# First-layer weights in two column halves, and one cast between two masks, in a fused retention and bilinear FFN kernel

## Chip, cores, metric

One core of a Trainium2 chip. The metric is the device time of one execution in microseconds (us), the median of several. A second number, the span of a profile, is counted from the first to the last instruction; it is about 1.7 us less than the time of the same execution.

## The reference

```python
# q, k, v: (8 batches, 8 heads, 576 positions, 64), float32; w_a, w_b: (512, 1536); w_out: (1536, 512)
scores = (1 / 8) * q @ k.T                            # per batch and head
D      = gamma_h ** (i - j) where i >= j, else 0      # gamma_h = 1 - 2 ** (-5 - h)
x      = (scores * D) @ v                             # heads side by side: (4608 tokens, 512)
out    = ((x @ w_a) * (x @ w_b)) @ w_out              # float32, (4608, 512)
```

## The kernel before

The tokens go through in 36 chunks of 128. Retention runs chunkwise: the decay is split into factors for q (applied to the output) and for v (applied when v is cast), and a running `state` carries the earlier chunks. The FFN runs in blocks of 512, 256, 384, 384, then 512 tokens. Chunks 0 to 3 are done first, in a prologue; the work of all later chunks is woven into the stream of FFN products at fixed places, counted in products of 512 columns.

The weights come by GpSimd DMAs that cast float32 to bf16 on the way, wa and wb in three pieces of 3, 4 and 5 column tiles of 128:

```python
def load_w(f0, f1):
    nc.gpsimd.dma_start(wa_sb[:, :, f0:f1], wa_r[:, :, f0:f1])
    nc.gpsimd.dma_start(wb_sb[:, :, f0:f1], wb_r[:, :, f0:f1])

def cast(i, on="pool"):                     # q, k to bf16; v to bf16 with its decay
    # [...] q on ScalarE (or GpSimd)
    if on == "dve":
        nc.vector.tensor_copy(kb, kf)
    else:
        nc.gpsimd.tensor_copy(kb, kf)
    nc.gpsimd.tensor_tensor(vb, vf, vs[...], op=ALU.mult)      # shapes cut

def scores(i):
    # [...] eight products into two PSUM tiles, then two masks, put off into `later`:
    later.append(lambda: masked(0))         # sT[:, 0] = ps[0] * mask, on VectorE
    later.append(lambda: masked(1))

# the prologue
for i in range(4):
    if idle[i][0]:
        warm(idle[i][0])                    # products without a use, which keep TensorE busy
    scores(i)
    flush()                                 # both masks
    if i == 2:
        load_w(0, W1)
        load_w(W1, W2)
    if i < 3:
        cast(i + 1, "dve" if i == 2 else "act")
    state(i)                                # needs vb of chunk i
    if idle[i][1]:
        warm(idle[i][1])
    if i < 3:
        transposes(i + 1)                   # needs q and k of chunk i+1 in bf16
        outputs(i)                          # needs both masks of chunk i; VectorE scales it into xT
        flush()
load_w(W2, DFF)
for i in (0, 1, 2):
    load_wo(i)
outputs(3, halves=True)
flush()
nc.sync.dma_start(gate, wo_sb[0:1, 3, 0:64])     # holds the loads behind it until W_out's first part is there
for i in range(4, 9):
    load(i)
```

In block 0 the products follow the pieces: with `WCOLS = [3, 4, 5]`, three column tiles of x·wa, the same three of x·wb, then four and four, then five and five. Each x·wa tile is copied to `ha` by ScalarE, and VectorE multiplies it with the x·wb tile into hT. All other blocks alternate wa and wb tile by tile.

Of the kernel before, what the change touches and what calls it, by code (L numbers as in the profile page):

```python
# [18 lines left out]
def kernel(  # L19
# [19 lines left out]
    nc = tc.nc  # L39
# [3 lines left out]
    DFF = moe_w_a.shape[1]  # L43
    NTOK = B * S
    NC = DM // 128
    NF = DFF // 128
# [19 lines left out]
    def pool(name, bufs, space=None):  # L66
        kw = {} if space is None else {"space": space}
        return ctx.enter_context(tc.tile_pool(name=name, bufs=bufs, **kw))
# [5 lines left out]
    qkt_pool = pool("qkt", 6)  # L74
    st_pool = pool("st", 4)
    h_pool = pool("hT", 2)
    ha_pool = pool("ha", 6)
    o_pool = pool("osb", 4)
    PS = bass.MemoryType.PSUM
    ps_ffn = pool("ps_ffn", 3, PS)  # L80
# [5 lines left out]
    wa_r = moe_w_a.rearrange("(c p) f -> p c f", p=128)  # L86
    wb_r = moe_w_b.rearrange("(c p) f -> p c f", p=128)
    wo_r = moe_w_out.rearrange("(c p) m -> p c m", p=128)
    wa_sb = big.tile([128, NC, DFF], BF16)
    wb_sb = big.tile([128, NC, DFF], BF16)  # L90
# [69 lines left out]
        nc.vector.memset(t, 0.0)  # L160

    def load_w(f0, f1):
        nc.gpsimd.dma_start(wa_sb[:, :, f0:f1], wa_r[:, :, f0:f1])
        nc.gpsimd.dma_start(wb_sb[:, :, f0:f1], wb_r[:, :, f0:f1])

    def load_wo(i):
        nc.gpsimd.dma_start(wo_sb[:, 4 * i:4 * i + 4, :],
# [6 lines left out]
    def pop():  # L174
        if later:
            later.pop(0)()

    def flush():
        while later:
            later.pop(0)()  # L180

    def cast(i, on="pool"):

        qf, kf, vf = staged.pop(i)
        qkb = nat.tile([128, 2, DM], BF16, tag="qkb", name="qkb")
        vb = nat.tile([128, DM], BF16, tag="vb", name="vb")
        qb, kb = qkb[:, 0], qkb[:, 1]
        if on == "pool":
            nc.gpsimd.tensor_copy(qb, qf)  # L189
        else:  # L190
            nc.scalar.copy(qb, qf)  # L191
# [4 lines that stand above are left out]
        nc.gpsimd.tensor_tensor(  # L196
            vb.rearrange("p (h d) -> p h d", h=H),
            vf.rearrange("p (h d) -> p h d", h=H),
            vs[:, i % PER, :].unsqueeze(2).to_broadcast([128, H, D]),
            op=ALU.mult)  # L200
        natural[i] = (qkb, qb, kb, vb)
# [9 lines left out]
    def transposes(i):  # L211

        natural_qk = natural[i][1:3]
        qkT = qkt_pool.tile([128, 2, HP, 128], BF16, tag="qkT", name="qkT")
        for w, copy in ((0, nc.scalar.copy), (1, nc.vector.tensor_copy)):
            tp = ps_att.tile([128, HP, 128], BF16, tag="att", name="tp")
            for p in range(HP):
                nc.tensor.transpose(tp[:, p, :],  # L218
                                    natural_qk[w][:, p * 128:(p + 1) * 128],
                                    identity)  # L220
            copy(qkT[:, w], tp)
        transposed[i] = qkT

    def state(i):
        m = i % PER
        if m == PER - 1:
            return
        qkb, qb, kb, vb = natural[i]
        r = slice(64, 128) if m == MID else slice(0, 128)
        if m == 0 or m == MID:  # L230
            kv_of[0] = ps_kv.tile([128, HP, 128], FP32, tag="kv", name="kv")
        kv = kv_of[0]
        for p in range(HP):
            sl = slice(p * 128, (p + 1) * 128)
            nc.tensor.matmul(kv[:, p, :], kb[r, sl], vb[r, sl],  # L235
                             start=(m in (0, MID) and p == 0), stop=True,
                             skip_group_check=True)
        st = states[i % len(states)]
        state_of[i + 1] = st
        nc.scalar.copy(st[0:64, :, 0:64], kv[0:64, :, 0:64])  # L240
        nc.scalar.copy(st[64:128, :, 64:128], kv[64:128, :, 64:128])

    def scores(i):
        qkT = transposed[i]
        ps = [ps_att.tile([128, HP, 128], FP32, tag="att", name=f"sc{hi}")
              for hi in (0, 1)]
        sT = st_pool.tile([128, 2, HP, 128], BF16, tag="sT", name="sT")
        scored[i] = sT
        for p in range(HP):
            for hi in (0, 1):  # L250
                r = slice(64 * hi, 64 * hi + 64)
                nc.tensor.matmul(ps[hi][:, p, :], qkT[r, 1, p, :],  # L252
                                 qkT[r, 0, p, :], start=True, stop=True,
                                 skip_group_check=True)
        keep = mask2 if i % PER == MID else mask

        def masked(hi):
            nc.vector.tensor_tensor(
                sT[:, hi], ps[hi],
                keep.unsqueeze(1).to_broadcast([128, HP, 128]),  # L260
                op=ALU.mult)

        later.append(lambda: masked(0))
        later.append(lambda: masked(1))

    def outputs(i, halves=False):
        m = i % PER
        qkb, qb, kb, vb = natural.pop(i)
        qkT = transposed.pop(i)
        sT = scored.pop(i)  # L270
        o = ps_att.tile([128, HP, 128], FP32, tag="att", name="o")
        if m > 0:
            st = state_of.pop(i)
            n = 64 if m == MID else 128
            for p in range(HP):
                for hi in (0, 1):
                    nc.tensor.matmul(o[64 * hi:64 * hi + 64, p, 0:n],  # L277
                                     st[:, p, 64 * hi:64 * hi + 64],
                                     qkT[:, 0, p, 0:n],
                                     start=(p == 0), stop=True,  # L280
                                     skip_group_check=True)
        for p in range(HP):
            for hi in (0, 1):
                e0 = p * 128 + 64 * hi
                nc.tensor.matmul(o[64 * hi:64 * hi + 64, p, :],  # L285
                                 vb[:, e0:e0 + 64], sT[:, hi, p, :],
                                 start=(m == 0 and p == 0), stop=True,
                                 skip_group_check=True)
        s0 = rows_of(i)[0][3]

        def scaled(c0, c1):
            nc.vector.tensor_tensor(  # L292
                xT[:, c0:c1, i * 128:(i + 1) * 128], o[:, c0:c1],
                qs[:, c0:c1, s0:s0 + 128], op=ALU.mult)

        if halves:
            later.append(lambda: scaled(0, HP // 2))
            later.append(lambda: scaled(HP // 2, HP))
        else:
            later.append(lambda: scaled(0, HP))  # L300


    blocks = [512, 256, 384, 384] + [512] * ((NTOK - 1536) // 512)
    WCOLS = [3, 4, 5]

    def ffn_block(tok0, n, runs):

# [60 lines left out]
    def warm(count):  # L368

        w = ps_ffn.tile([128, 4, 128], FP32, tag="ab", name="w")  # L370
        for _ in range(count):
            nc.tensor.matmul(w, identity,  # L372
                             identity.unsqueeze(1).to_broadcast([128, 4, 128]),
                             start=True, stop=True)

    W1, W2 = 128 * WCOLS[0], 128 * (WCOLS[0] + WCOLS[1])
    idle = {0: (0, 0), 1: (0, 3), 2: (2, 4), 3: (1, 4)}
    make_qs(0)
    make_qs(1)
# [4 lines left out]
    for i in range(4):  # L384
        if idle[i][0]:
            warm(idle[i][0])
        scores(i)
        flush()
        if i == 2:
            load_w(0, W1)  # L390
            load_w(W1, W2)
        if i < 3:
            cast(i + 1, "dve" if i == 2 else "act")
        state(i)
        if idle[i][1]:
            warm(idle[i][1])
        if i < 3:
            transposes(i + 1)
            outputs(i)
            flush()  # L400
    load_w(W2, DFF)
    for i in (0, 1, 2):
        load_wo(i)
    outputs(3, halves=True)
# [77 lines left out]
    at = 0.0  # L482
    tok = 0
    for tb, n in enumerate(blocks):
        runs = WCOLS if tb == 0 else [1] * NF
        for cost, edge in ffn_block(tok, n, runs):
            at += cost
            while todo and edge and at >= todo[0][0]:
                _, fn, args = todo.pop(0)
                fn(*args)  # L490
        flush()
        tok += n
# [30 lines left out]
```

## Time and profile before

| | us |
|---|---|
| median of three executions | 345.88 (345.83 to 346.28) |
| the execution that was profiled | 879.55, span 877.8 |

The first thing to read is that the profile is not a picture of the timed runs: the profiled execution took two and a half times as long. From the page of the kernel before, its span, its busy times and TensorE's row of the span in 40 slices (busy share in tenths):

```profile
span 877.8 us, 6134 instructions
...
PE 854.0 (97%) x2390; PEld 309.4 (35%) x2426; DVE 162.0 (18%) x272; ACT 112.6 (13%) x229; POOL 84.3 (10%) x121
...
PE   6999999999999999999999999999999999999998
```

TensorE (PE) seems full, and the summary of the chain of waits agrees (share of the span by engine):

```profile
PE 97%; issue 2%; DMA 1%; SPq 0%; POOL 0%; DVE 0%; ACT 0%
```

But the pace is wrong. From the same chain in order of time (start, duration, what), 20 products of block 0, each with 512 columns:

```profile
62.97 11.87 PE pa L316 x20
```

That is 0.59 us per product. The FFN has 1296 of these (nine times 512 tokens; per 512 tokens 12·4 for wa, 12·4 for wb and 48 for W_out), which alone makes over 760 us at this pace and cannot fit into 346. So every TensorE duration of this profile is useless for the timed runs.

What it does show is when the weights come. From the DMA issues of the kernel before (bytes as written in bf16, and us from issue to landing):

```profile
wa_sb<-in_moe_w_a_dram POOLq DMA_DIRECT2D x1, 640.0 KB, 12.0
wb_sb<-in_moe_w_b_dram POOLq DMA_DIRECT2D x1, 640.0 KB, 14.2
wa_sb<-in_moe_w_a_dram POOLq DMA_DIRECT2D x1, 512.0 KB, 8.9
wb_sb<-in_moe_w_b_dram POOLq DMA_DIRECT2D x1, 512.0 KB, 10.6
...
wa_sb<-in_moe_w_a_dram POOLq DMA_DIRECT2D x1, 384.0 KB, 6.0
wb_sb<-in_moe_w_b_dram POOLq DMA_DIRECT2D x1, 384.0 KB, 7.0
```

and GpSimd in order of time, from vb of chunk 2 to vb of chunk 3:

```profile
14.12 1.04 POOL L196 TENSOR_TENSOR vb<-vf,vs 128x512 bf16<-128x512 f32 x1 [0.61 <-DMA vf<-in_v_dram]
15.11 0.95 POOL L163 DMA_DIRECT2D wa_sb<-in_moe_w_a_dram  x1
16.05 0.76 POOL L164 DMA_DIRECT2D wb_sb<-in_moe_w_b_dram  x1
16.79 0.76 POOL L163 DMA_DIRECT2D wa_sb<-in_moe_w_a_dram  x1
17.52 0.77 POOL L164 DMA_DIRECT2D wb_sb<-in_moe_w_b_dram  x1
18.28 1.08 POOL L196 TENSOR_TENSOR vb<-vf,vs 128x512 bf16<-128x512 f32 x1
```

Adding the issue times gives landings of wa at 21.1, 25.7, 31.3 us and of wb at 23.0, 28.1, 34.5 us. Each weight DMA holds GpSimd for about 0.75 us, and vb of chunk 3 stands behind four of them.

### The profile page before, as it was taken

The page shows a single profiled execution, that of the slowest core. Times are in us where ns is not written, and L with a number is a line of the kernel's source. Part 1 is how long each engine was busy: PE and PEld are TensorE (multiplying, and loading weights), DVE is VectorE, ACT ScalarE, POOL GpSimd, SP SyncE. Part 2 cuts the span into 40 slices and gives each one's busy share as a digit, 9 for nine tenths or more (in the row PEclk, how much of TensorE's full clock was granted, in tenths as well). Part 3 has the DMA queues.
Part 4 walks back from the last instruction along what each step waited for, and adds up shares of the span by engine and source line. Part 5 has one row for each costly group of instructions (what it writes and reads, how often), then busy time and mean ns, then how long its engine had stood idle before and what let it go on. Part 6 is the DMA issues. An engine that isn't in the chain of part 4 may idle for free.

```text
span 877.8 us, 6134 instructions
## 1 busy us (share of the span) xinstructions
PE 854.0 (97%) x2390; PEld 309.4 (35%) x2426; DVE 162.0 (18%) x272; ACT 112.6 (13%) x229; POOL 84.3 (10%) x121
## 2 busy tenths in 40 slices
PE   6999999999999999999999999999999999999998
PEld 3322345344344333333333333432333333232223
DVE  4211122222121111211122112121121112201100
ACT  5111112011011101100111011101110011101110
POOL 6040002201011010002100210011000000000000
DMA  9980049350090041025400650066002300000000
GB/s 181 207 152 0 25 90 187 80 88 1 29 199 0 13 102 18 0 50 108 81 1 1 131 108 1 0 112 129 0 1 60 61 0 1 8 28 12 0 13 36
DMA packets 154333, 50.74 MB, mean 58 GB/s; under 512 B 144960, under 2 KB 149824, under 8 KB 154304
## 3 DMA queue, kind: packets, MB, share of 16 engines
q1 hardware_dynamic: 149552, 45.63, 26.6%
q0 software_dynamic: 4752, 4.72, 3.4%
q8 instruction: 19, 0.31, 0.2%
q14 instruction: 10, 0.08, 0.0%
HBM read 37.75 MB, written 9.44 MB: 54 GB/s over the span
## 4 chain that ended last, share of the span: by engine, by line
PE 97%; issue 2%; DMA 1%; SPq 0%; POOL 0%; DVE 0%; ACT 0%
PE pb L329 29%; PE pa L316 29%; PE po L349 28%; PE o L285 2%; PE kv L235 2%; PE o L277 2%; PE w L372 1%; PE tp L218 1%; DMA kf<-in_k_dram 1%; SPq L104 0%; POOL qkb L195 0%; PE sc_2460 L252 0%; PE sc_2449 L252 0%; PE sc_1402 L252 0%; PE sc_3677 L252 0%
## 5 line engine op out<-in xcount | busy, mean ns | idle before, releaser
L329 PE MATMUL pb<-xT,wb_sb 128*128 128x512 bf16 (+2 forms) x471 | 279.9, 775 | 2.7 <-issue 2.7
L316 PE MATMUL pa<-xT,wa_sb 128*128 128x512 bf16 (+2 forms) x472 | 277.3, 769 | 3.6 <-issue 3.1
L349 PE MATMUL po<-wo_sb,hT 128*128 128x512 bf16 (+1 forms) x425 | 253.2, 810 | 6.2 <-issue 6.2
L334 DVE TENSOR_TENSOR hT<-ha,pb 128x512 bf16<-128x512 bf16 (+2 forms) x120 | 76.2, 635 | 457.4 <-PE pb L329 443.3
L329 PEld LDWEIGHTS <-wb_sb 128*128 128x128 bf16 x480 | 82.8, 172 | 173.7 <-issue 168.0
L316 PEld LDWEIGHTS <-wa_sb 128*128 128x128 bf16 x480 | 80.7, 172 | 157.2 <-issue 151.4
L349 PEld LDWEIGHTS <-hT 128*128 128x128 bf16 x444 | 73.1, 169 | 162.1 <-issue 159.0
L322 ACT CAST ha<-pa 128x512 bf16<-128x512 f32 (+2 forms) x120 | 65.2, 544 | 447.1 <-PE pa L316 440.9
L196 POOL TENSOR_TENSOR vb<-vf,vs 128x512 bf16<-128x512 f32 x36 | 37.6, 1044 | 295.1 <-issue 144.3
L189 POOL CAST qkb<-qf 128x512 bf16<-128x512 f32 x30 | 18.3, 611 | 290.5 <-DMA qf<-in_q_dram 274.6
L360 DVE COPY osb<-po 128x512 f32<-128x512 f32 (+1 forms) x17 | 11.5, 676 | 175.5 <-PE po L349 175.5
L358 ACT COPY osb<-po 128x512 f32<-128x512 f32 (+1 forms) x20 | 11.5, 576 | 219.3 <-PE po L349 208.4
L292 DVE TENSOR_TENSOR xT<-o,qs 128x512 bf16<-128x512 f32 (+1 forms) x37 | 24.8, 674 | 46.8 <-PE o L285 46.8
L285 PE MATMUL o<-sT,vb 128*64 128x128 bf16 x288 | 30.4, 379 | 0.0
L235 PE MATMUL kv<-vb,qkb 128*128 128x128 bf16 (+1 forms) x128 | 25.4, 373 | 1.4 <-issue 0.9
L235 PEld LDWEIGHTS <-qkb 128*128 128x128 bf16 (+1 forms) x128 | 17.6, 161 | 22.2 <-issue 20.9
L285 PEld LDWEIGHTS <-vb 128*64 128x64 bf16 x288 | 22.3, 181 | 2.5 <-issue 2.5
L195 POOL CAST qkb<-kf 128x512 bf16<-128x512 f32 x32 | 19.7, 616 | 13.6 <-DMA kf<-in_k_dram 13.5
L252 PEld LDWEIGHTS <-qkT 64*128 64x128 bf16 x288 | 15.4, 135 | 12.6 <-issue 9.8
L218 PE MATMUL tp<-identity,qkb 128*128 128x128 bf16 x48 | 8.1, 362 | 6.0 <-ACT qkb L191 5.3
L372 PE MATMUL w<-identity 128*128 128x512 bf16 x14 | 9.3, 790 | 0.0
L218 PEld LDWEIGHTS <-qkb 128*128 128x128 bf16 x48 | 5.2, 140 | 11.1 <-ACT qkb L191 5.7
(195 smaller groups left out, 194.7 us busy)
## 6 DMA issues: line engine op xcount, KB each, us to landing
out_dram<-osb SPq DMA_DIRECT2D x35, 256.0 KB, 2.2
qf<-in_q_dram SPq DMA_DIRECT2D x32, 256.0 KB, 3.6
kf<-in_k_dram SPq DMA_DIRECT2D x32, 256.0 KB, 4.2
vf<-in_v_dram SPq DMA_DIRECT2D x32, 256.0 KB, 4.7
wo_sb<-in_moe_w_out_dram POOLq DMA_DIRECT2D x3, 512.0 KB, 17.8
qf<-in_q_dram SPq DMA_DIRECT2D x8, 128.0 KB, 3.6
kf<-in_k_dram SPq DMA_DIRECT2D x8, 128.0 KB, 3.5
vf<-in_v_dram SPq DMA_DIRECT2D x8, 128.0 KB, 3.5
```

Source lines behind the costliest of these rows:

```text
L189: nc.gpsimd.tensor_copy(qb, qf)
L195: nc.gpsimd.tensor_copy(kb, kf)
L196: nc.gpsimd.tensor_tensor(vb.rearrange("p (h d) -> p h d", h=H), vf.rearrange("p (h d) -> p h d", h=H), vs[:, i % PER, :].unsqueeze(2).to_ ...
L218: nc.tensor.transpose(tp[:, p, :], natural_qk[w][:, p * 128:(p + 1) * 128], identity)
L235: nc.tensor.matmul(kv[:, p, :], kb[r, sl], vb[r, sl], start=(m in (0, MID) and p == 0), stop=True, skip_group_check=True)
L285: nc.tensor.matmul(o[64 * hi:64 * hi + 64, p, :], vb[:, e0:e0 + 64], sT[:, hi, p, :], start=(m == 0 and p == 0), stop=True, skip_group_che ...
L292: nc.vector.tensor_tensor(xT[:, c0:c1, i * 128:(i + 1) * 128], o[:, c0:c1], qs[:, c0:c1, s0:s0 + 128], op=ALU.mult)
L316: nc.tensor.matmul(pa[:, 0:n], wa_sb[:, c, fs], xT[:, c, tok0:tok0 + n], start=(c == 0), stop=(c == NC - 1))
L322: nc.scalar.copy(ha[:, 0:n], pa[:, 0:n])
L329: nc.tensor.matmul(pb[:, 0:n], wb_sb[:, c, fs], xT[:, c, tok0:tok0 + n], start=(c == 0), stop=(c == NC - 1))
L334: nc.vector.tensor_tensor(hT[:, F, 0:n], has[F][:, 0:n], pb[:, 0:n], op=ALU.mult)
L349: nc.tensor.matmul(po[:, 0:width], hT[:, F, u * 128:(u + 1) * 128], wo_sb[:, F, cols], start=(F == 0), stop=(F == NF - 1))
```

## The change

Its intent, as the few words that came with it and the code show: load wa and wb in two halves, so that GpSimd has four weight DMAs to issue and not six; let only three of them stand ahead of vb of chunk 3; run block 0 as six wa tiles, six wb tiles, and again; and cast k of chunk 3 on VectorE between the two masks of chunk 2, so that its transposes can begin earlier. `ha` gets a seventh buffer for the longer run.

```diff
-    ha_pool = pool("ha", 6)
+    ha_pool = pool("ha", 7)
 [...]
     def load_w(f0, f1):
-        nc.gpsimd.dma_start(wa_sb[:, :, f0:f1], wa_r[:, :, f0:f1])
-        nc.gpsimd.dma_start(wb_sb[:, :, f0:f1], wb_r[:, :, f0:f1])
+        for w_sb, w_r in ((wa_sb, wa_r), (wb_sb, wb_r)):
+            nc.gpsimd.dma_start(w_sb[:, :, f0:f1], w_r[:, :, f0:f1])
+            yield
 [...]
-    WCOLS = [3, 4, 5]
+    WRUN = NF // 2
 [...]
         scores(i)
-        flush()
+        pop()
         if i == 2:
-            load_w(0, W1)
-            load_w(W1, W2)
-        if i < 3:
-            cast(i + 1, "dve" if i == 2 else "act")
+            list(load_w(0, W1))
+            second = load_w(W1, DFF)
+            next(second)
+        if i == 2:
+            cast(3, "dve")
+            flush()
+        else:
+            flush()
+            if i < 3:
+                cast(i + 1, "act")
 [...]
-    load_w(W2, DFF)
+    list(second)
 [...]
-        runs = WCOLS if tb == 0 else [1] * NF
+        runs = [WRUN] * 2 if tb == 0 else [1] * NF
```

The built instruction streams differ in just these places: the order of block 0's products, one cast and one mask swapped on VectorE, and GpSimd's DMAs.

More of the change, by code (lines that the diff above doesn't have):

```diff
@@ L374, in warm @@
                              start=True, stop=True)
-    W1, W2 = 128 * WCOLS[0], 128 * (WCOLS[0] + WCOLS[1])
+    W1 = 128 * WRUN
     idle = {0: (0, 0), 1: (0, 3), 2: (2, 4), 3: (1, 4)}
```

## The prediction

> **What bounds the kernel now.** The profile is unlike the timed runs: its span is 877.8 us, the timed median 345.88. The chain of waits is 97% TensorE, and block 0's products with 512 columns follow each other every 0.60 us (20 in 11.87 us). The FFN has 1296 such products: at 0.60 us they alone would be 778 us. The Trainium skill ("TensorE: Matmul & The Clock Gate", Back-to-back gap and its table) gives about 216 ns at full clock; 1296 of those are 280 us, which fits the timed runs. So I take matmul times from the skill, and every DMA, VectorE, ScalarE and GpSimd time from the trace. Timed runs are TensorE-bound too, except in the prologue (chunks 0 to 3), which is a chain of loads, casts, copies and masks. The change touches only that and block 0; later blocks keep their instruction order.
>
> **Weights, from the DMA issues and landings in the trace.** wa lands in pieces of 3, 4, 5 column tiles at 21.1, 25.7 and 31.3 us, wb at 23.0, 28.1 and 34.5; W_out at 37.0 to 42.3. Bytes flow at a steady ~207 GB/s, so landing is set by bytes ahead in the queue, not by TensorE.
>
> **Adds, removes, moves.**
> 1. Two of six GpSimd DMA issues go (0.76 us each). In the timeline vb of chunk 3 starts at 18.28 us after four issues, though its load landed at 17.4; after three issues it starts at about 17.5. State of chunk 3, the last four warming matmuls and the output of chunk 3 follow it: up to 0.75 us earlier.
> 2. VectorE: k of chunk 3 is cast (0.42 us) between two masks (0.6 us spacing). That can bring its transposes 0.6 us forward, but its load lands only at about 16.5 us (issue at 11.29 plus 5.2). With fast matmuls the first mask ends before that, I estimate, and VectorE then waits for the load with the second mask behind it: between 0.5 us gained and 0.35 us lost.
> 3. The first product now needs 768 KB of wa (bf16 as written) in place of 384 KB. These bytes were wa's and wb's first pieces together, landing at 23.0; with larger packets I expect 22.6 to 23.0.
> 4. The second half of the run order costs nothing: wb half 1 lands at ~26.9, wanted at ~28; wa half 2 at ~30.7, wanted at ~33.
>
> **Critical path.** Working through the prologue with full-clock matmuls I estimate block 0 starts at 21.5 us before (at half clock 22.9). After, attention would be ready at about 20.7 (22.1), but wa holds it until about 22.7. So block 0 starts 1.2 us later (or 0.2 us earlier), and everything behind moves with it.
>
> **Predicted time:** 346.4 us, range 344.9 to 347.9. Faster by over 2%: 1%; within 2%: 98%; slower by over 2%: 1%. Within that, slightly slower is likelier (65%).
>
> **What would show it.** wa's first landing near 22.8 us; vb of chunk 3 starting near 17.5; the VectorE cast of k waiting for its DMA or directly behind the first mask; at a fast clock the first pa product waiting for wa's DMA instead of the xT multiply. In a profile as slow as this one (block 0 starts at 29.5 us, well after the weights) the wait cannot appear, and the span should hardly change.
>
> **What would make it wrong.** A timed prologue longer than I estimate (block 0 starting after 23 us): then points 1 and 2 are real gains of 0.3 to 0.75 us. A larger first transfer ramping up faster. Or an idle TensorE that drops its clock at block 0, costing 1 to 2 us more.

## More of the kernel before

From chunk 6 on, q and k are transposed by DMA (`turn`), and the places of chunks 6 to 10 are:

```python
placed = [((6, 7), 145, 178, 194), ((8,), 166, 197, 207), ((9, 10), 186, 224, 254)]
# chunks: where the casts are issued, where the scores stand, where the outputs stand
```

## The result, and the profile after

| | kernel before | changed kernel |
|---|---|---|
| median, us | 345.90 (4 runs, 345.83 to 346.28) | 345.97 (4 runs, 345.51 to 347.08) |
| ratio | | 1.0004, 95% interval 0.998 to 1.0029 |

A ratio is the mean time of one kernel's fast runs over that of the other's fast runs of the same rounds, so it is not quite the ratio of the medians. The interval says: the same, within 0.3%, which is 1 us. Nearly all effects below are of that size or smaller, so most of the evidence is in the traces, not in the times.

The profile of the changed kernel fell in a fast execution (347.08 us), so TensorE's pace can now be read:

```profile
span 345.4 us, 6131 instructions
...
PE 328.0 (95%) x2390; PEld 171.8 (50%) x2426; DVE 160.8 (47%) x272; ACT 112.4 (33%) x229; POOL 83.5 (24%) x119
```

The chain of waits of the changed kernel around the start of block 0 (start, duration, what):

```profile
13.66 0.99 POOL vb L197
14.65 7.15 DMA wa_sb<-in_moe_w_a_dram
21.80 0.04 issue
21.84 0.39 PE pa L317
22.23 0.05 issue
22.29 4.91 PE pa L317 x22
```

The first product of block 0 waits for wa's half, which was issued at 14.65 us and lands at 21.80 us. The 22 products after it come every 0.22 us, so TensorE is at full clock. No VectorE or GpSimd step is in this chain any more between vb of chunk 2 and the first product. GpSimd in order of time shows that the intended gain is there: vb of chunk 3 stands behind three issues and starts at 17.15 us.

```profile
16.33 0.76 POOL L164 DMA_DIRECT2D wa_sb<-in_moe_w_a_dram  x1
...
17.15 1.04 POOL L197 TENSOR_TENSOR vb<-vf,vs 128x512 bf16<-128x512 f32 x1
```

VectorE in order of time has the cast of k between the two masks:

```profile
15.52 0.69 DVE L259 TENSOR_TENSOR sT<-sc_305,mask 128x512 bf16<-128x512 f32 x1 [0.17 <-PE sc_306 L253]
...
16.13 0.47 DVE L194 CAST qkb<-kf 128x512 bf16<-128x512 f32 x1
...
16.52 0.67 DVE L259 TENSOR_TENSOR sT<-sc_306,mask 128x512 bf16<-128x512 f32 x1
```

And these are TensorE's waits for DMAs in the whole changed kernel (us in total, times, longest):

```profile
PE pa L317 <- DMA wa_sb<-in_moe_w_a_dram: 1.7, 1, 1.7
PE sc_1216 L253 <- DMA qkT<-qkb: 1.4, 1, 1.4
...
PE sc_1399 L253 <- DMA qkT<-qkb: 0.7, 1, 0.7
...
PE sc_1111 L253 <- DMA qkT<-qkb: 0.5, 1, 0.5
```

The last three lines are the ones that I had not looked for: scores of chunks 8, 10 and 12 waited 2.6 us for DMA transposes, at 72, 80 to 82 and 94 us.

To follow a delay through the kernel I use the 120 hT multiplies of VectorE: they stand in each trace in the same order, and the start of the n-th in one trace less that of the n-th in another is the lag at this point. The lag below is always against the fast profile of the kernel before that the first experiment brought.

### The profile page after: what moved, and what is told of

Its sections match the earlier page's. It is cut to its first block, busy times and chain, and to the rows that moved or that the text cites. A ratio compares the mean times of both kernels' runs of the same rounds, so it can differ in the third digit from the quotient of the medians.

```text
span 345.4 us, 6131 instructions
## 1 busy us (share of the span) xinstructions
PE 328.0 (95%) x2390; PEld 171.8 (50%) x2426; DVE 160.8 (47%) x272; ACT 112.4 (33%) x229; POOL 83.5 (24%) x119
## 4 chain that ended last, share of the span: by engine, by line
PE 82%; DMA 11%; SPq 4%; issue 2%; POOL 1%; ACT 0%; POOLq 0%
PE po L350 25%; PE pa L317 25%; PE pb L330 24%; DMA vf<-in_v_dram 3%; DMA qf<-in_q_dram 3%; SPq L104 3%; DMA wa_sb<-in_moe_w_a_dram 2%; PE o L278 2%; PE o L286 2%; PE kv L236 2%; DMA qkT<-qkb 1%; SPq L207 1%; POOL vb L197 1%; DMA out_dram<-osb 1%; POOL qkb L190 0%
## 5 line engine op out<-in xcount | busy, mean ns | idle before, releaser
L317 PE MATMUL pa<-xT,wa_sb 128*128 128x512 bf16 (+2 forms) x471 | 110.5, 358 | 2.4 <-DMA wa_sb<-in_moe_w_a_dram 1.7
L330 PE MATMUL pb<-xT,wb_sb 128*128 128x512 bf16 (+2 forms) x472 | 110.6, 357 | 0.4
L350 PE MATMUL po<-wo_sb,hT 128*128 128x512 bf16 (+1 forms) x425 | 96.2, 373 | 1.5 <-issue 0.8
L330 PEld LDWEIGHTS <-wb_sb 128*128 128x128 bf16 x480 | 47.0, 98 | 46.5
L317 PEld LDWEIGHTS <-wa_sb 128*128 128x128 bf16 x480 | 45.0, 98 | 45.1 <-DMA wa_sb<-in_moe_w_a_dram 1.9
L350 PEld LDWEIGHTS <-hT 128*128 128x128 bf16 x444 | 41.6, 98 | 45.9
L286 PE MATMUL o<-sT,vb 128*64 128x128 bf16 x288 | 14.5, 222 | 0.2 <-DVE sT L259 0.2
L236 PE MATMUL kv<-vb,qkb 128*128 128x128 bf16 (+1 forms) x128 | 12.8, 224 | 0.3
L236 PEld LDWEIGHTS <-qkb 128*128 128x128 bf16 (+1 forms) x128 | 9.4, 99 | 6.6 <-issue 1.7
L286 PEld LDWEIGHTS <-vb 128*64 128x64 bf16 x288 | 10.2, 111 | 1.4 <-issue 1.3
```

What stands on the lines that cost most here:

```text
L236: nc.tensor.matmul(kv[:, p, :], kb[r, sl], vb[r, sl], start=(m in (0, MID) and p == 0), stop=True, skip_group_check=True)
L286: nc.tensor.matmul(o[64 * hi:64 * hi + 64, p, :], vb[:, e0:e0 + 64], sT[:, hi, p, :], start=(m == 0 and p == 0), stop=True, skip_group_che ...
L317: nc.tensor.matmul(pa[:, 0:n], wa_sb[:, c, fs], xT[:, c, tok0:tok0 + n], start=(c == 0), stop=(c == NC - 1))
L330: nc.tensor.matmul(pb[:, 0:n], wb_sb[:, c, fs], xT[:, c, tok0:tok0 + n], start=(c == 0), stop=(c == NC - 1))
L350: nc.tensor.matmul(po[:, 0:width], hT[:, F, u * 128:(u + 1) * 128], wo_sb[:, F, cols], start=(F == 0), stop=(F == NF - 1))
```

## The experiments

Two theories:

- A, the one that I predicted with: the start of block 0 passes one to one to the end.
- B: a second stream sets the pace up to about 95 us. The loads of q, k, v for chunks 4 and on, their casts and their DMA transposes arrive when they arrive, TensorE gets there early and waits, and so a shift of block 0's start is swallowed (if late) or refunded (if early) as long as it is smaller than those waits.

Twelve runs were made: x1 repeats the kernel before, z3 the changed kernel, and z2 the version of x4. All gave correct results. Each trace shows one execution.

### x1: the kernel before, unchanged

> The kernel before, unchanged, against itself: the noise floor, and a profile of it at full TensorE clock, which is missing so far. Theory A (mine: the start of block 0 passes one to one to the end): block 0 starts about 0.7 us earlier than the 21.84 us of the changed kernel, at about 21.1 us, and waits there for the xT multiply or just for wa. Theory B (a second chain, made of q, k, v loads, casts and DMA transposes for chunks 6 and on, sets when TensorE gets through about 80 to 95 us, whenever block 0 started): block 0 starts earlier too, but the waits for DMA transposes at 80 to 95 us add up to more than the 2.6 us seen in the changed kernel, so that by 100 us the two kernels are level within 0.3 us. Ratio 1.000 within 0.002 either way.

Measured: 346.28 us median against 346.28, ratio 0.9993 (0.9974 to 1.0012): two sets of runs of one kernel agree within 0.2%. The profile is fast, and its chain shows how the kernel before really starts block 0:

```profile
14.89 0.88 POOL wa_sb L163
15.77 0.74 POOL wb_sb L164
16.51 0.74 POOL wa_sb L163
17.24 0.74 POOL wb_sb L164
17.99 1.08 POOL vb L196
...
19.11 0.38 PE kv L235 x4
19.50 0.86 PE w L372 x4
...
20.97 0.44 DVE xT L292
...
21.45 0.38 PE pa L316
```

(The products of the output lie in the gap before the xT multiply at 20.97 us.) This is the prologue of the prediction: four weight issues hold GpSimd, then vb of chunk 3, its state product, four warming products, the output, the xT multiply, and block 0 at 21.45 us (my estimate was 21.5). wa's first piece had landed at 20.00 us. The changed kernel starts at 21.84 us, so the change costs 0.39 us there (about 0.7 was expected). TensorE's waits for DMA transposes in this trace:

```profile
PE sc L252 <- DMA qkT<-qkb: 2.4, 3, 1.4
```

Expected under B were longer waits for transposes and level kernels by 100 us. The waits are 2.4 us, not more than the changed kernel's 2.6, and the lag at the end is 0.61 us. So this pair of traces alone fits A as well as B. It takes the others.

### x2: three pieces again, with the other two ideas kept

Against the changed kernel, with lines joined; the runs of 3, 4 and 5 tiles and the six `ha` buffers are those of the kernel before:

```diff
-            list(load_w(0, W1)); second = load_w(W1, DFF); next(second)
+            list(load_w(0, W1)); second = load_w(W1, W2); next(second)   # pieces of 3, 4, 5
 [...]
-    list(second)
+    list(second); list(load_w(W2, DFF))
```

> The changed kernel with three pieces (3, 4, 5) again, but its two other ideas kept: three weight issues ahead of vb of chunk 3, and k of chunk 3 cast between the masks. wa's first piece should land at about 20.7 us instead of 21.8 and block 0 start at about 20.8. Theory A: about 1.0 us faster than the changed kernel and 0.3 us faster than the kernel before (ratio 0.999 to it). Theory B: block 0 starts early all the same, and the time is that of the kernel before within 0.3 us.

Measured: ratio 1.0001 (0.998 to 1.0021), median 346.59 us. wa's first piece landed at 20.13 us and block 0 started at 21.01 us, 0.44 us earlier than in the kernel before and 0.83 us earlier than in the changed kernel. The lead was there at the end of block 0 (lag -0.43 us). It was gone later: TensorE waited 3.0 us for transposes, and the end lagged by 0.46 us. The scores of chunk 10 show it: they began when their transpose had landed, in x1 at 81.36 us and in x2 at 81.82 us, whatever block 0 had done. First x1, then x2:

```profile
81.41 0.40 PE L252 MATMUL sc<-qkT 64*128 64x128 bf16 x8 [1.35 <-DMA qkT<-qkb]
...
81.86 0.40 PE L253 MATMUL sc<-qkT 64*128 64x128 bf16 x8 [1.33 <-DMA qkT<-qkb]
```

In this trace A is wrong: a lead did not arrive. The times alone do not decide it, as the interval holds A's forecast (0.999) too.

### x3: wb's half ahead of wa's half

```diff
-        for w_sb, w_r in ((wa_sb, wa_r), (wb_sb, wb_r)):
+        for w_sb, w_r in ((wb_sb, wb_r), (wa_sb, wa_r)):
```

> The changed kernel with wb's half loaded ahead of wa's half: same bytes, same issues, other order. The first product of block 0 should wait until about 25.5 us, 3.7 us later than in the changed kernel; nothing after it should wait for weights. Theory A: 3.7 us slower than the changed kernel (ratio to before about 1.010 to 1.012). Theory B: the delay is eaten by the DMA transpose waits at 80 to 95 us, of which there are 2.6 us in the changed kernel: 1 to 2 us slower, and those waits shrink to near nothing.

Measured: 350.95 us median, ratio 1.0127 (1.0104 to 1.015), 4.4 us slower by that ratio. The first product started at 25.82 us, as planned. Both theories missed a part that the trace shows. In stretches of the trace, the first number after the comma is PE's busy time, and PEclk is the granted clock, behind the busy times:

```profile
20.00:25.80 5.80, 0.29 (x12) 0.13 (x6) 0.76 (x2) 0.00 (x0) 1.42 (x2) 0.86 1.15 208
25.80:30.00 4.20, 3.96 (x9) 1.50 (x11) 0.00 (x0) 1.14 (x2) 0.00 (x0) 0.50 1.16 210
30.00:35.00 5.00, 5.00 (x22) 2.19 (x21) 0.34 (x1) 2.38 (x5) 0.00 (x0) 0.90 1.19 207
```

After 5.5 us of waiting, TensorE's clock was halved for the first 4 us of block 0 and part of the next 5. The lag grew from 4.37 us at the first product to 6.90 us at the end of block 0. From there it shrank to 4.67 us, where it stayed to the end: 2.23 us were swallowed, and TensorE waited for no transposes at all in this run. So the sum is 4.37 (late start) + 2.53 (half clock) - 2.23 (swallowed) = 4.67. Theory B gets the swallowing right, but its total was wrong because the clock was left out. A's total (1.010 to 1.012) came near by luck: it left out the half clock and the swallowing, which almost cancel.

The trace also shows that the second stream is not independent of block 0. In SyncE's queue, block 0's four output stores stand ahead of the transposes of chunks 6 and 7. In x1 the last store was issued at 59.35 us, 2.1 us after its data were ready (57.23 us); so I estimate from these two times that block 0 could be about 2.1 us late before it holds the transposes back. In x3 these data were ready only at 64.04 us. SyncE's issues at this place, first in x1, then in x3:

```profile
60.10 3.26 SPq L206 DMA_TRANSPOSE qkT<-qkb  x2
...
64.06 0.33 SPq L362 DMA_DIRECT2D out_dram<-osb  x1
64.50 2.76 SPq L207 DMA_TRANSPOSE qkT<-qkb  x2
```

So in x3 the stream itself came 4.40 us later. No run changed the order of this queue.

### x4 and z2: halves and earlier vb, but the cast behind both masks

Lines joined:

```diff
-        pop()
+        flush()
 [...]
-        if i == 2:
-            cast(3, "dve"); flush()
-        else: [...]
+        if i < 3:
+            cast(i + 1, "dve" if i == 2 else "act")
```

> The two halves and the earlier vb of chunk 3 without the new order of the k cast. Block 0 must start where the changed kernel starts (21.8 us), for both theories, because wa's first half sets it; the ratio to before is that of the changed kernel within noise (1.000 to 1.003). If instead the cast order matters, block 0 starts at another time.

Measured: ratio 0.9994 (0.9974 to 1.0015), median 346.20 us. But block 0 did not start at wa's landing (22.01 us): it started at 22.68 us, released by the xT multiply. VectorE's cast of k had taken 1.08 us in place of 0.42:

```profile
17.41 1.04 POOL L197 TENSOR_TENSOR vb<-vf,vs 128x512 bf16<-128x512 f32 x1
...
17.65 1.08 DVE L194 CAST qkb<-kf 128x512 bf16<-128x512 f32 x1
...
18.79 0.40 PE L219 MATMUL tp<-identity,qkb 128*128 128x128 bf16 x4 [0.96 <-DVE qkb L194]
```

The cast began 0.24 us after GpSimd's vb of chunk 3 and ended 0.28 us after it, and the transposes waited 0.96 us. The Trainium skill, page "SBUF — State Buffer", section "Who interferes with whom", says that VectorE's copies and casts can, in some modes, use a port pair which GpSimd shares, and that whoever comes second is then blocked for the whole instruction of the other. The numbers agree with it roughly: a cast that does nothing until vb ends at 18.45 us and then takes its full 0.42 us would end at 18.87, and it ended at 18.73. That the port pair is the cause is not shown by an experiment of its own. In this trace, then, the earlier vb and the cast overlap. In the changed kernel, with the cast ahead of the second mask, they do not (the cast starts at 16.13 us there, vb at 17.15 us).

A second look:

> Second look at the halves without the new cast order. In the first look the k cast of chunk 3 took 1.08 us on VectorE in place of 0.42 while GpSimd made vb of chunk 3, and block 0 started at 22.68 us, but the masks before it were late (TensorE at half clock in its prologue). If the two collide whenever the cast begins after vb, the cast is long only if the masks are late again; with masks on time the cast begins at about 16.4 us, ahead of vb at 17.4, takes 0.42 us, and block 0 starts at wa's landing, 22.0 us. In both cases the end should lag the kernel before by what the DMA transposes at 81 us lag, within 0.3 us, and not by the start of block 0.

Measured: 346.48 us, one run. The masks were late again (first mask at 16.47 us, in the kernel before at 15.23), the cast began at 17.68 us behind vb at 17.35, took 1.01 us, and block 0 started at 22.64 us (wa had landed at 22.50). That is the first case of the expectation. The collision has been seen twice and not once without late masks, so whether it goes away with masks on time stays open. A trace made for another question tells what the new cast order does when masks are late: y2 below has that order and its first mask at 16.34 us; its cast began at 16.95 us, ahead of vb at 17.40, took 0.63 us, and block 0 started at 22.04 us, at wa's landing (22.00). The end of z2 lagged by 0.01 us, though block 0 had ended 1.19 us late. In x4 the lag fell from 1.23 to -0.38 us, and its scores of chunk 10, too, began when their transpose landed:

```profile
81.04 0.40 PE L253 MATMUL sc<-qkT 64*128 64x128 bf16 x8 [0.46 <-DMA qkT<-qkb]
```

These two traces are the plainest evidence for B: over a microsecond of delay at block 0 was swallowed whole.

### y1, y2, y3: the scores of chunks 6 to 12 placed later

If B holds, placing these scores later should make the waits go away and the kernel faster.

```diff
-    placed = [((6, 7), 145, 178, 194), ((8,), 166, 197, 207),
-              ((9, 10), 186, 224, 254)]
+    placed = [((6, 7), 145, 182, 196), ((8,), 166, 200, 208),
+              ((9, 10), 186, 236, 264)]
 [...]
-        placed.append((g, third - 104, third - (30 if i == 11 else 36), third))
+        placed.append((g, third - 104, third - (22 if i == 11 else 36), third))
```

On the kernel before:

> The kernel before with the scores (and what follows them) of chunks 6 to 12 placed later in the stream of products, so that TensorE no longer arrives before their DMA transposes. In the first batch TensorE waited 2.4 us for these in the kernel before, 3.0 with the small first piece, 1.1 with halves only, 0 with wb first. Theory B (these waits swallow or refund a shift of block 0's start): the waits fall to under 0.5 us and the kernel is about 2 us faster than before (ratio 0.993 to 0.996). Theory A (no second limit; those waits are incidental): ratio 1.000 within 0.002, other waits appear in place of these.

Measured: ratio 0.9994 (0.9978 to 1.001), median 346.14 us. The 2 us that B expected did not come: in time the result is the one named under A (1.000 within 0.002, other waits in place of these). The waits of TensorE:

```profile
PE o L285 <- DVE sT L258: 0.9, 2, 0.5
...
PE sc L252 <- DMA qkT<-qkb: 0.7, 2, 0.5
```

Waits for transposes fell from 2.4 to 0.7 us, but outputs now waited 0.9 us for masks (0.2 in the kernel before), as they stand closer behind their scores. With block 0 starting 0.20 us later in this execution, 0.8 us should be left of the gain; the trace ends 0.38 us earlier. The other 0.4 us I have not traced. So part of what B promised turned into a new wait, and B's claim that removing the waits makes the kernel faster is not borne out by this run.

On the changed kernel:

> The changed kernel with the same later scores. Theory B: also about 2 us faster than the changed kernel, and since nothing absorbs it any more, its lag behind the kernel before with later scores is its later start of block 0 (0.4 us in the profiles so far) all the way to the end: 0.1 to 0.8 us slower than that. Theory A: level with the changed kernel.

Measured: ratio 1.0011 (0.9992 to 1.0031), median 346.70 us, 0.56 us above y1. In the traces, y2 started block 0 0.39 us after y1, lagged it by 0.41 us at the end of block 0, and by 0.31 us at the end. No scores waited for transposes in y2. That the later start arrives where the slack is gone is what B said of the difference. But the intervals of y1 and y2 overlap, a start that always passes to the end (A) would give the same 0.4 us, and B's 2 us over the changed kernel did not come. This pair does not decide between the two.

On x2's version (small first piece, early vb, cast between masks):

> Three pieces, early vb, cast between masks, and later scores: the version that should beat all if theory B holds, because its earlier start of block 0 (0.43 us in the profile) is no longer lost: ratio to before 0.991 to 0.995, and 0.4 us ahead of the kernel before with later scores. Theory A: ratio 0.999 to 1.001.

Measured: ratio 0.9987 (0.9975 to 0.9999), median 346.14 us, level with y1. In the trace its block 0 ran 0.78 us ahead of y1's and its end was 0.05 us behind: at 66 us the scores of chunk 7 waited 0.8 us for their transpose. The lead was refunded again. B's ratio of 0.991 to 0.995 was missed; the result lies just outside A's 0.999.

### y4: only the cast order

> The kernel before with only the k cast of chunk 3 moved between the masks of chunk 2. vb of chunk 3 then still starts at about 18 us and holds the state product, so block 0 should start within 0.15 us of the 21.45 us of the kernel before, and the ratio is 1.000 within 0.002. If the cast order were worth something by itself, block 0 would start 0.3 us or more earlier. The cast must take 0.42 us here, not the 1.08 us that it took in the run with halves only, where vb of chunk 3 ran on GpSimd at the same time.

Measured: ratio 0.9991 (0.9978 to 1.0004), median 346.46 us. Block 0 started at 21.47 us, 0.02 us off, and the cast took 0.56 us: longer than the 0.42 that I had demanded, but half of what it took under the collision. The cast order by itself gained nothing at the start of block 0 in this trace, because the state product still waited for vb, as long as before (0.68 us against 0.59).

### z1: chunks 6, 7 and 8 later too

```diff
-    placed = [((6, 7), 145, 182, 196), ((8,), 166, 200, 208),
+    placed = [((6, 7), 145, 188, 201), ((8,), 166, 202, 210),
```

> The small first piece with early vb, cast between masks, and the scores of chunks 6 to 12 later, now those of chunks 6, 7 and 8 too, where the previous version of it waited 0.8 us for a DMA transpose and lost its 0.78 us lead over the kernel before with later scores. Theory B (the stream of loads and DMA transposes sets the end, and only a wait for it refunds a lead): either that wait goes and the lead of 0.5 to 0.8 us arrives at the end (ratio to before 0.996 to 0.998), or the wait moves to the next transposes and the ratio stays at 0.998 to 1.000. Theory A: the lead was a fluke of one execution, ratio 0.9987 as the last version.

Measured: ratio 0.9996 (0.998 to 1.0012), median 346.61 us. The wait of chunk 7 is gone, and a new one stands where block 2 begins, because its last xT is now ready too late:

```profile
77.01 0.81 PE L317 MATMUL pa<-xT,wa_sb 128*128 128x384 bf16 x4 [1.38 <-DVE xT L293]
```

The lead of 0.55 us shrank to 0.18. Other placements that I built, with the outputs of chunks 9 and 10 still later, ended in a deadlock in the simulator and did not go to the chip (by my own account). No version that I tried beats the kernel before by more than the noise; y3 is the nearest, at 0.13%, with an interval that all but touches 1, and the best of several that were compared.

### z3: the changed kernel again

> Second look at the changed kernel: the first product waits for wa's DMA again (0.5 to 1.8 us), starts at 21.8 to 22.1 us, 0.4 to 0.6 us after the kernel before, and the end lags the profile of the kernel before by what the DMA transposes at about 81 us lag (theory B), not by the lag of block 0's start (theory A).

Measured: 347.09 us, one run. The first product waited 2.04 us for wa, longer than expected, and started at 22.29 us, 0.84 us after the kernel before. This time the clock fell too, with 24 products in 7.04 us where full clock takes 5.3 (z2). The first five products still ran at full clock; the granted clock was half from 23.50 to 26.91 us:

```profile
22.29 7.04 PE L317 MATMUL pa<-xT,wa_sb 128*128 128x512 bf16 x24 [2.04 <-DMA wa_sb<-in_moe_w_a_dram]
```

At the end of block 0 the lag was 2.54 us; 0.61 us were left of it at the end, and no scores waited for transposes. So 1.93 us were swallowed. The expectation that the end would lag as the transposes do was wrong for this run (those of chunk 10 were issued at 76.50 us, 0.10 us before the kernel before): TensorE was so late that it set its own pace.

### z4: the loads of chunks 4 to 8 let go later

```diff
-    nc.sync.dma_start(gate, wo_sb[0:1, 3, 0:64])
+    nc.sync.dma_start(gate, wo_sb[0:1, 7, 0:64])
```

> The kernel before with the loads of chunks 4 to 8 let go one W_out piece later: 38.4 us in place of 35.9 us. Block 0 starts as before (21.45 us within 0.2). Theory B: the stream of loads is what sets the end, so a good part of the 2.5 us arrives: 0.5 to 2.5 us slower (ratio 1.002 to 1.007), with longer waits of TensorE for transposes. Theory A: the start of block 0 is unchanged, so the time is too (1.000 within 0.002).

Measured: ratio 1.0014 (0.9993 to 1.0035), median 347.31 us, 0.65 us above the median of before: on the slow side, but below the 1.002 that B expected and not clear of the noise. In the trace block 0 started at 21.51 us, TensorE waited 3.4 us for transposes, and the end lagged by 0.96 us with no lag at all in block 0. SyncE let the loads go 2.59 us later than in x1 and issued the transpose of chunk 6 0.95 us later. So a part of a shift that was made in the stream of loads alone arrived, in one trace.

### All traces side by side

The nine full-pace traces with the scores at their old places (in y1, y2, y3 and z1 chunk 10 stands elsewhere). z2 and z3 are single executions, so their state is unknown; the others are fast. Lags against x1, in us. "Chunk 10" is the start of the scores of chunk 10, which stood at 81.41 us in x1; "waits" is the time for which TensorE waited for DMA transposes.

| run | first product | lag, end of block 0 | waits | lag, chunk 10 | lag, end |
|---|---|---|---|---|---|
| x1, before | 21.45 | 0 | 2.4 | 0 | 0 |
| changed | 21.84 | 0.41 | 2.6 | 0.59 | 0.61 |
| z3, changed again | 22.29 | 2.54 | 0 | 0.62 | 0.61 |
| x2, small first piece | 21.01 | -0.43 | 3.0 | 0.45 | 0.46 |
| x4, halves only | 22.68 | 1.23 | 1.1 | -0.37 | -0.38 |
| z2, halves only again | 22.64 | 1.19 | 1.3 | -0.03 | 0.01 |
| y4, cast order only | 21.47 | 0.02 | 2.4 | 0.11 | 0.10 |
| z4, late loads | 21.51 | 0.06 | 3.4 | 0.97 | 0.96 |
| x3, wb first | 25.82 | 6.90 | 0 | 4.68 | 4.68 |

The last two columns agree within 0.04 us in every row, and the column of block 0 predicts neither of them until it passes about 2 us. In the seven rows with waits, the scores of chunk 10 began when their DMA transpose landed. Two executions of one version differ too: x4 and z2 by 0.39 us at the end. So lags of this size in single traces carry little by themselves; what carries the argument is which wait ended last.

## Why the prediction was right, and where it was not

The time was predicted at 346.4 us (344.9 to 347.9) and came at 345.97. The interval of the ratio is about 1 us wide to each side, so the times confirm "the same" and cannot confirm a loss of 0.5 us. Point by point:

1. The timed runs are at full clock: right. 24 products took 5.18 us in the chain of the changed kernel, 0.216 us each. The Trainium skill, page "TensorE: Matmul & The Clock Gate", section "Back-to-back issue gap", gives this figure for isolated products of 512 columns, and 131 ns for a real stream with weight loads. Here a stream with weight loads ran at the first figure, not at the second.
2. vb of chunk 3 at about 17.5 us: right, 17.15 us in a trace in which GpSimd's first issue was 0.46 us earlier than in the profile that I read.
3. The start of block 0 in the kernel before: right, 21.45 us against 21.5, set by the chain that I named (x1).
4. wa's half would hold the changed kernel: right in kind. It was sized at 1.2 us later than before and measured 0.39 and 0.84 us in two traces. I had taken about 7.6 us from issue to landing; it was 7.15 and 7.37 us, and the issue came earlier as well.
5. The cast between the masks, "between 0.5 us gained and 0.35 us lost": 0.02 us by itself (y4). I missed what it does in this change: when the masks are late, it keeps the cast out of the way of the earlier vb (y2 against x4 and z2). With masks on time this was not tested.
6. "So block 0 starts 1.2 us later (or 0.2 us earlier), and everything behind moves with it": this is the step that failed. Up to a delay of about 2 us, the scores of some of the chunks 7 to 12 wait for DMA transposes anyway (2.4 us in x1), and SyncE's queue has about as much room; only what goes beyond passes on (4.68 of 6.90 us in x3). A delay of 1.2 us was swallowed (x4, z2), a lead of 0.4 us was refunded (x2), and a part of a shift of the loads alone arrived (z4).
7. An idle TensorE that drops its clock, named as a risk at 1 to 2 us: it happened in one of the two traces of the changed kernel, at 1.7 us (the lag grew from 0.84 to 2.54 us in block 0), and was mostly swallowed too.

So the total was near for a partly wrong reason: a small loss was predicted to arrive, but a later start of block 0, which varies from run to run, is mostly absorbed. That the number came so near is luck. What the change removes (0.75 us of GpSimd issue on the chain) is real, but it is paid for at once by the larger first transfer, and neither reaches the end at its size. That delays are swallowed and leads refunded is shown by the waits in the traces of x4, z2, z3 and x2. That the later start arrives once the slack is placed away (y2 against y1: 0.31 us in the traces, 0.56 in the medians) is within the noise. What moves the stream of loads and transposes by up to 0.6 us between traces whose block 0 was less than 2 us late is open.

## What to carry to other kernels

Before costing a change at one point, follow its lag downstream: look for the next place where the same engine waits for a stream that does not depend on that point, because this wait swallows a delay and refunds a lead up to about its own size. Check how independent that stream is: here one queue joined the two, because the stores of the early block stood ahead of the later transposes. Cutting the first loads into fewer, larger pieces to save issues moved the wait here from the issuing engine to the first consumer; size the first piece by what the consumer needs first. And when a profile's time is far from the timed runs, use it for what still runs at pace (loads, other engines) and get a second profile before believing anything about the slow engine.

## What the Trainium skill lacked or had wrong

- "TensorE: Matmul & The Clock Gate", section "What's actually happening", gives the half clock after at least one idle window of about 3.4 us. In z3 TensorE stood idle for 2.04 us, ran five products at full clock, and was then at half clock from 23.50 to 26.91 us; in the 3.41 us before the drop it had been busy for about 1.4. In the changed kernel's first profile it stood idle for 1.74 us and kept full clock. So an idle time well under 3.4 us was enough once, the drop came after the work had begun again, and two executions of one kernel differed. The recovery cost 1.7 us here and 2.5 us in x3.
- The same page knows half clock and full clock (and a third state under load from other cores). The first profile of the kernel before ran its products at 0.59 us each, which is slower than half clock (twice 0.216 us), through a span of 877.8 us. Its granted clock is given as 1.0, but its page has no PEclk row, so the clock was not recorded. The page mentions cold products of 617 ns on average in one kernel and a clock stuck at a quarter for over 50 us; it explains neither, and no page explains a whole execution at this pace. Nor did its 131 ns for a real stream show in any run (point 1 above).
- "SBUF — State Buffer", section "Who interferes with whom", agrees roughly with the collision of the cast with vb (1.08 and 1.01 us in place of 0.42). It could add that the blocked instruction's time in the profile includes the blocking, so that it shows as a long cast and not as a gap.
- No page gives the time of a casting GpSimd DMA with other loads still in the queues ahead of it: 768 KB (as written) took 7.10 to 7.61 us from issue to landing in five traces (changed, z3, x4, z2, y2), 384 KB 5.17 to 5.63 us in seven others (x1, x2, y1, y3, y4, z1, z4).
